# Scores and row maxima made one slot earlier in a fused threshold attention and gated MLP kernel

## The chip, the cores and the metric

The kernel runs on one core of a Trainium2 chip. The metric is the time of one execution on the device, in microseconds (us), taken as the median of several runs. Smaller is better.

## What is computed

The first half is attention over 8 batches of 8 heads, with 576 positions and a head size of 64, in which every score that lies more than `tau` below its row's maximum is thrown away before the softmax. The second half is a gated two-layer MLP on the 4608 rows that come out. The types are float32 at both ends.

```
def _attn_ref(q, k, v, tau):
    scale = 1.0 / np.sqrt(q.shape[-1])
    scores = scale * np.matmul(q, k.transpose(0, 1, 3, 2))
    thresh = np.max(scores, axis=-1, keepdims=True) - tau
    scores = np.where(scores >= thresh, scores, -1000000000.0)
    scores = scores - np.max(scores, axis=-1, keepdims=True)
    attn = np.exp(scores)
    attn = attn / (np.sum(attn, axis=-1, keepdims=True) + 1e-09)
    return np.matmul(attn, v).astype(np.float32)

def _moe_ref(x, w_in, w_out):          # x: [4608, 512], w_in: [512, 2048], w_out: [2048, 512]
    h = x @ w_in
    relu6 = np.clip(h + 3.0, 0.0, 6.0)
    g = h * relu6 / 6.0
    return (g @ w_out).astype(np.float32)
```

## The kernel before, in words

**Tiles.** Four heads make a *quad*, so there are 16 quads, two to a batch. A quad has nine *slots*: slots 0 to 3 are the four blocks of 128 query rows of its first pair of heads, slots 4 to 7 those of its second pair, and slot 8 holds the 64 left-over rows of all four heads. One slot is 128 rows by 576 keys for two heads. The loop runs over the 144 slots in order (`n` counts them), and each engine gets its instructions in the order in which this loop writes them: the schedule is written by hand, there is no planner. An engine works through its own list in order, so an instruction that waits holds up all that stand behind it.

**One pass of the loop** (slot `n`) writes, in this order:

- ScalarE: `sm_exp` (L315) of slot n-1, two heads;
- VectorE: `sm_max` (L302) of slot n, which copies the scores out of PSUM and takes their row maxima; GpSimd: the two `bias` values (L305) made from the maxima;
- TensorE: `mm1` (L378), the first MLP product of one item, into `ps_h`; then its relu (L387 on ScalarE or L389 on VectorE, chosen by slot through `on_act`) and its gate (L395, VectorE), which empties `ps_h`. Slot 8 has no `mm1`. An item is 320 columns wide (a *wide* slot) or 256 (a *narrow* one);
- TensorE, in the first 21 slots, for every second slot: `pe_transpose` of the weights of slot n-2, copied out by VectorE (L340);
- VectorE: `sm_recip` (L318) of slot n-1;
- TensorE: a quarter of an output tile (`mm2_part`, L407); the fourth quarter is followed by `osb` on VectorE (L415), which empties the one bank of `ps_o`;
- ScalarE: `sm_mask` (L310) of slot n, which needs the bias of slot n;
- by slot: transposes of queries and keys that later slots need, or `av_main` (L348) or `av_rest`. Queries are transposed by VectorE (L239) and keys too (L245) from quad 4 on; in quads 0 to 3 TensorE transposes them and VectorE or ScalarE copies them out (L237, L218, L220);
- TensorE: `scores` (L281, L287) of slot n+1;
- GpSimd: `sm_norm` (L323) of slot n-1; SyncE: the DMA transpose (L331) of its result;
- SyncE: a few loads of coming queries and keys, and finished output rows (L428); GpSimd: a few loads with a cast (weights, and values).

From quad 1 on the slot-dependent part was: second pair's queries in slot 1, its keys in slot 2, `av_main` in slots 3 and 8, `av_rest` in slot 4, the next quad's queries, keys and left-over rows in slots 5, 6 and 7.

**Buffers around the change.** The pool `ps_s` has two tiles of two PSUM banks each, and a slot's scores take both; so `scores` of one slot wait until `sm_max` of the slot before has read. `ps_h` has one tile: `mm1` of a slot waits for the gate of the slot before. The copy of the scores in SBUF (`s_pool`) has four buffers, and `sm_max` writes into one that `sm_norm` must have read. The DMA transposes and the loads stand in one list on SyncE.

**Start and end.** Before the loop, the first scores are made. During the first 22 slots there is no MLP work. After the loop, the rest of the MLP runs (`rest1`, `rest2`), with relu on ScalarE.

Of the kernel before, what the change touches and what calls it, by code (L numbers as in the profile page):

```python
# [21 lines left out]
def kernel(  # L22
# [17 lines left out]
    NQUAD = B * H // 4  # L40
    NSLOT = 9
    NB = 2
# [90 lines left out]
    def load_v(b):  # L133
        vm = v_pool.tile([P, H, 4 * D], BF16, tag="vm", name="vm")
        vr = vrs[b % 2]
        vsb[b] = (vm, vr)
        for g in range(2):
            vcasts.append(lambda g=g: nc.gpsimd.dma_start(
                out=vm[:, g * 4:g * 4 + 4, :],
                in_=v[b, g * 4:g * 4 + 4, 0:512, :].rearrange("h (p t) d -> p h (t d)", t=4)))  # L140
        for a in range(2):
            vcasts.append(lambda a=a: nc.gpsimd.dma_start(
                out=vr[a * 64:(a + 1) * 64, a, :, :],
                in_=v[b, :, 512:S, :].rearrange("(hp a) p d -> a p hp d", a=2)[a]))
# [21 lines left out]
    def start(jobs, n):  # L166
        for _ in range(min(n, len(jobs))):
            jobs.pop(0)()
# [30 lines left out]
    def qT_of(pair):  # L199
        return qkT[pair // 2][0][:, pair % 2, :]  # L200
# [68 lines left out]
    def keys(pair, a, hf):  # L269
        kT = kT_of(pair)  # L270
        c0 = 64 * (1 - a) + hf * HALF
        return kT[a * 64:(a + 1) * 64, c0:c0 + HALF]


    def scores(quad, slot):
        tiles = [ps_s.tile([P, 2, 512], F32, tag="s", name="s") for _ in range(2)]
        for hf in range(2):
            if slot < 8:
                pair, t = 2 * quad + slot // 4, slot % 4
                for a in range(2):  # L280
                    nc.tensor.matmul(tiles[a][:, hf, 0:HALF], qT_of(pair)[a * 64:(a + 1) * 64, t * P:(t + 1) * P],  # L281
                                     keys(pair, a, hf), start=True, stop=True)
            else:
                for n in range(2):
                    for a in range(2):
                        pair = 2 * quad + n
                        nc.tensor.matmul(tiles[a][n * 64:(n + 1) * 64, hf, 0:HALF],  # L287
                                         qT_of(pair)[a * 64:(a + 1) * 64, 512:S], keys(pair, a, hf),
                                         start=True, stop=True)
        return tiles  # L290
# [4 lines left out]
    def sm_max(sl):  # L295
        sl.s = s_pool.tile([P, 2, S], F32, tag="s", name="s")
        sl.m = stat_pool.tile([P, 2], F32, tag="m", name="m")
        sl.bias = stat_pool.tile([P, 2], F32, tag="bias", name="bias")
        sl.rsum = stat_pool.tile([P, 2], F32, tag="rsum", name="rsum")
        sl.rinv = stat_pool.tile([P, 2], F32, tag="rinv", name="rinv")  # L300
        for i, ps in enumerate(sl.tiles):
            nc.vector.tensor_scalar(out=sl.s[:, i, :].rearrange("p (a b) -> p a b", a=2), in0=ps[:, :, 0:HALF],  # L302
                                    scalar1=1.0, scalar2=None, op0=Alu.mult, op1=Alu.max,
                                    accum_out=sl.m[:, i:i + 1])
            nc.gpsimd.tensor_scalar(out=sl.bias[:, i:i + 1], in0=sl.m[:, i:i + 1], scalar1=-scale, scalar2=tau,  # L305
                                    op0=Alu.mult, op1=Alu.add)
# [6 lines left out]
    def sm_exp(sl, i):  # L313
        s = sl.s[:, i, :]
        nc.scalar.activation(out=s, in_=s, func=Act.Exp, accum_out=sl.rsum[:, i:i + 1])  # L315

    def sm_recip(sl):
        nc.vector.reciprocal(out=sl.rinv[:], in_=sl.rsum[:])  # L318
# [54 lines left out]
    def mm1(item, pool=None):  # L373
        b, ni, c0, w = item
        hps = (pool or ps_h).tile([P, 2, 512], F32, tag="s" if pool else "h", name="h")
        for n in range(2):
            for ki in range(KI):
                nc.tensor.matmul(hps[:, n, 0:w], w_in_sb[:, ki, (ni + n) * P:(ni + n + 1) * P],  # L378
                                 xT[b][:, ki, c0:c0 + w], start=(ki == 0), stop=(ki == KI - 1))
        return hps[:, :, 0:w]  # L380


    def mm1_relu(hps, on_act):
        w = hps.shape[2]
        r = r_pool.tile([P, 2, 320], F32, tag="r", name="r")[:, :, 0:w]
        if on_act:
            nc.scalar.activation(out=r, in_=hps, func=Act.Relu, bias=three[:])  # L387
        else:
            nc.vector.tensor_scalar(out=r, in0=hps, scalar1=3.0, scalar2=0.0, op0=Alu.add, op1=Alu.max)  # L389
        return r  # L390

    def mm1_gate(item, hps, r):
        b, ni, c0, w = item
        c0 += (b % 2) * S
        nc.vector.scalar_tensor_tensor(out=gbuf[:, ni:ni + 2, c0:c0 + w], in0=r, scalar=6.0, in1=hps,  # L395
                                       op0=Alu.min, op1=Alu.mult)
# [63 lines left out]
    queue = []  # L460
    for quad in range(NQUAD):
        for slot in range(NSLOT):
            sl = Slot()
            sl.quad, sl.slot = quad, slot
            sl.on_chip = len(queue) < N1 - 1 and len(queue) % 2 == 1
            queue.append(sl)
    queue[0].tiles = scores(0, 0)

    prev = None
    for n, sl in enumerate(queue):  # L470
        quad, slot = sl.quad, sl.slot
        b, g = divmod(quad, 2)
        now = n
        if slot in (0, 4):
            pts[2 * quad + slot // 4] = pt_pool.tile([P, 9, 512], BF16, tag="pT", name="pT")
        if slot == 8:
            ptr[quad] = ptr_pool.tile([P, 9, P], BF16, tag="pR", name="pR")
        if quad == 0 and slot == 0:
            load_quad(1)
        if slot == (4 if quad else 8) and quad + 2 < NQUAD:  # L480
            load_quad(quad + 2)
        if slot == 0 and g == 1 and b + 1 < B:
            load_v(b + 1)
        if prev is not None:
            for i in range(2):
                sm_exp(prev, i)
        sm_max(sl)

        if slot != 8 and todo1:
            item, then = todo1.pop(0)  # L490
            h = mm1(item)
            r = mm1_relu(h, on_act=(slot in ((1, 2, 3, 5, 6) if quad >= 2 * NB else (0, 1, 3, 5))))
            mm1_gate(item, h, r)
            todo2.extend(then)
        copies = pe_transpose(queue[n - 2]) if n > 1 and queue[n - 2].on_chip else None
        if prev is not None:
            sm_recip(prev)
        if copies:
            copies()
        outs = []  # L500


        pieces = 0 if slot == 3 else 1
        if slot == 0:
            second = True
        if second and slot < 2 and len(todo2) > 1 and todo2[0][1] == todo2[1][1]:
            pieces, second = 2, False
        for _ in range(pieces):
            if todo2:
                bb, mt, part = todo2.pop(0)  # L510
                mm2_part(bb, mt, part)
                if part == 3:
                    outs += mm2_out(bb, mt, on_act=False)
        for i in range(2):
            sm_mask(sl, i)
        evict = None
        nxt = 2 * quad + 2
        if slot == 1:
            evict = transpose_q(2 * quad + 1)
        elif slot == 2:  # L520
            evict = transpose_k(2 * quad + 1)
        elif n == 3:
            evict = transpose_rest(0, of_k=False)
        elif slot == 3 and quad > 0:
            av_main(2 * quad - 1)
        elif slot == 4 and quad > 0:
            av_rest(quad - 1)
            if quad % 2 == 0:
                todo1.extend(moe_of(quad // 2 - 1))
        elif slot in (5, 6, 7) and quad + 1 < NQUAD:  # L530
            if slot == 5:
                alloc_qk(quad + 1)
                evict = transpose_q(nxt)
            elif slot == 6:
                evict = transpose_k(nxt)
            else:
                evict = transpose_rest(quad + 1)
        elif slot == 8:
            av_main(2 * quad)
        if evict:  # L540
            evict()
        if n == 0:
            warm_up(8)
        if n + 1 < len(queue):
            queue[n + 1].tiles = scores(queue[n + 1].quad, queue[n + 1].slot)
        if n < 8:
            warm_up(6)
        if prev is not None:
            sm_norm(prev)
        flush()  # L550
        late.extend(outs)
        if not 30 < n < 34:
            start(loads, 1)
        if n < 4 or 15 < n < 20 or n > 33:
            start(vcasts, 1)
        elif n > 3:
            start(casts, 2 if 21 < n < 29 else 1)
        prev = sl
# [80 lines left out]
```

## Time and profile before

| | us |
|---|---|
| median of 5 runs | 550.01 |
| lowest and highest run | 548.73, 553.34 |
| the profiled execution's own time | 548.73 |
| its span in the profile | 547.0 |

| engine | busy us (share of the span) |
|---|---|
| TensorE, matmuls | 524.1 (96%) |
| TensorE, weight loads | 299.3 (55%) |
| ScalarE (ACT) | 463.0 (85%) |
| VectorE (DVE) | 428.8 (78%) |
| GpSimd (POOL) | 305.1 (56%) |

The page comes from one profiled execution. PE is TensorE, and matmul ends are modelled: matmuls overlap, so a busy PE is not a PE at its peak. A line such as L302 is a line of the kernel. In the timeline each row has its start, its length, the engine (a q after it means the engine's sequencer, so SPq is SyncE issuing a DMA), the line, what is written and read, and in brackets the idle time of the engine before it, with what ended it. In the list of waits the three numbers are the total, how often, and the longest.

### The profile page before, as it was taken

How to read it: one execution, taken by the hardware profiler on the slowest of the kernel's cores; microseconds unless marked ns; L12 is line 12 of the kernel's file. 1: busy time of each engine (PE TensorE's matmuls, PEld its weight loads, DVE VectorE, ACT ScalarE, POOL GpSimd, SP SyncE). 2: the span in 40 equal slices, each digit the busy share in tenths (PEclk: the TensorE clock that was granted, in tenths of full speed). 3: DMA queues.
4: the chain of work that ended last, by engine and by line, in shares of the span. 5: the costliest groups of instructions: out<-in, count | busy, mean ns of one | idle time of the engine just before them, and what ended most of it. 6: DMA issues, size and time to landing. Idle time of an engine off the chain costs nothing.

```text
span 547.0 us, 11518 instructions
## 1 busy us (share of the span) xinstructions
PE 524.1 (96%) x3774; PEld 299.3 (55%) x3774; DVE 428.8 (78%) x1055; ACT 463.0 (85%) x986; POOL 305.1 (56%) x646
## 2 busy tenths in 40 slices
PE   8998898999999999899999999999999999999997
PEld 7755465545555555555555555555555565554663
DVE  3888886788888888788988888888988888874441
ACT  4999989988989898999889899899889899993440
POOL 2888888666566555654566555754566555561000
PEclk9999999999999999999999999999999999999999
DMA  6999989989999997998699778998689786653102
GB/s 122 137 132 181 183 123 185 181 143 166 158 157 173 136 168 139 177 155 165 114 143 189 142 156 141 176 164 155 131 135 190 138 153 107 123 110 86 40 19 78
DMA packets 311692, 77.52 MB, mean 142 GB/s; under 512 B 294608, under 2 KB 307152, under 8 KB 311632
## 3 DMA queue, kind: packets, MB, share of 16 engines
q1 hardware_dynamic: 293024, 67.47, 70.1%
q0 software_dynamic: 17408, 8.92, 14.0%
q8 instruction: 30, 0.49, 0.4%
q10 hardware_dynamic: 1200, 0.39, 0.3%
q14 instruction: 30, 0.25, 0.2%
HBM read 36.70 MB, written 9.44 MB: 84 GB/s over the span
## 4 chain that ended last, share of the span: by engine, by line
PE 59%; ACT 10%; DVE 7%; POOL 4%; DMA 3%; issue 3%; SPq 1%; DVEq 0%; POOLq 0%
PE o L407 18%; PE h L378 17%; PE s L281 16%; ACT s L310 4%; PE av L348 4%; ACT s L315 3%; DVE s L302 3%; POOL pn L323 2%; DMA pR<-pn 2%; ACT r L387 2%; PE s L287 2%; DVE g L395 1%; DVE r L389 1%; DMA km<-in_k_dram 1%; PE av L351 1%
## 5 line engine op out<-in xcount | busy, mean ns | idle before, releaser
L323 POOL TENSOR_SCALAR pn<-s,rinv 128x576 bf16<-128x576 f32 x288 | 211.6, 745 | 126.0 <-DVE rinv L318 60.9
L302 DVE TENSOR_SCALAR_CACHE_REDUCE s<-s 128x576 f32<-128x576 f32 x288 | 205.2, 749 | 30.6 <-PE s L281 22.4
L310 ACT ACTIVATE s<-s,bias 128x576 f32<-128x576 f32 x288 | 206.9, 766 | 26.3 <-POOL bias L305 25.9
L315 ACT ACTIVATE s<-s 128x576 f32<-128x576 f32 x288 | 192.4, 670 | 0.3
L281 PE MATMUL s<-kT,qT 64*128 64x288 f32 x1024 | 172.2, 430 | 4.5 <-DVE s L302 4.2
L378 PE MATMUL h<-xT,w_in_sb 128*128 128x320 bf16 (+1 forms) x1024 | 145.0, 287 | 3.6 <-DVE g L395 2.8
L407 PE MATMUL o<-w_out_sb,g 128*128 128x512 bf16 x576 | 140.9, 379 | 3.9 <-DVE osb L415 3.9
L281 PEld LDWEIGHTS s<-kT,qT 64*128 64x128 f32 x1024 | 96.0, 186 | 65.8 <-DVE s L302 34.6
L378 PEld LDWEIGHTS <-w_in_sb 128*128 128x128 bf16 x1024 | 91.7, 98 | 66.3 <-issue 38.1
L395 DVE SCALAR_TENSOR_TENSOR g<-r,h 128x512 bf16<-128x512 f32 (+1 forms) x128 | 96.3, 754 | 37.7 <-ACT r L387 36.3
L305 POOL TENSOR_SCALAR bias<-m 128x1 f32<-128x1 f32 x288 | 54.4, 189 | 62.5 <-DVE s L302 41.1
L407 PEld LDWEIGHTS <-g 128*128 128x128 bf16 x576 | 55.6, 98 | 58.3 <-issue 9.9
L387 ACT ACTIVATE r<-h,three 128x640 f32<-128x640 f32 (+1 forms) x86 | 62.8, 732 | 25.7 <-PE h L378 25.3
L315 ACT ACTIVATION_READ_ACCUMULATOR s<-s 128x1 f32 x288 | 54.1, 188 | 0.0
L415 DVE TENSOR_SCALAR osb<-o 128x512 f32<-128x512 f32 x31 | 20.9, 674 | 21.7 <-PE o L407 21.4
L348 PE MATMUL av<-pT,vm 128*64 128x512 bf16 x256 | 33.7, 385 | 1.1 <-DMA pT<-pn 1.1
L348 PEld LDWEIGHTS <-vm 128*64 128x64 bf16 x512 | 17.6, 110 | 26.4 <-issue 13.3
L389 DVE TENSOR_SCALAR r<-h 128x512 f32<-128x512 f32 (+1 forms) x42 | 31.5, 750 | 0.0
L318 DVE RECIPROCAL rinv<-rsum 128x2 f32<-128x2 f32 x144 | 22.9, 159 | 8.4 <-ACT s L315 7.7
L360 DVE CAST xT<-av 128x512 bf16<-128x512 f32 x32 | 21.8, 681 | 6.6 <-PE av L351 6.5
L302 DVE DVE_READ_ACCUMULATOR s<-s 128x1 f32 x288 | 23.9, 83 | 0.0
L287 PE MATMUL s<-kT,qT 64*64 64x288 f32 x256 | 21.3, 415 | 0.6 <-DVE s L302 0.6
(57 smaller groups left out, 218.6 us busy)
## 6 DMA issues: line engine op xcount, KB each, us to landing
out_dram<-osb SPq DMA_DIRECT2D x31, 256.0 KB, 2.6
nq<-in_q_dram SPq DMA_DIRECT2D x96, 72.0 KB, 3.1
km<-in_k_dram SPq DMA_DIRECT2D x96, 64.0 KB, 2.7
vm<-in_v_dram POOLq DMA_DIRECT2D x16, 256.0 KB, 5.3
km<-in_k_dram SPq DMA_DIRECT2D x16, 128.0 KB, 4.2
w_in_sb<-in_moe_w_in_dram POOLq DMA_DIRECT2D x16, 128.0 KB, 4.4
w_out_sb<-in_moe_w_out_dram POOLq DMA_DIRECT2D x16, 128.0 KB, 4.2
pT<-pn SPq DMA_TRANSPOSE x119, 3.7
```

The lines of the kernel that those rows point to most:

```text
L281: nc.tensor.matmul(tiles[a][:, hf, 0:HALF], qT_of(pair)[a * 64:(a + 1) * 64, t * P:(t + 1) * P], keys(pair, a, hf), start=True, stop=True)
L302: nc.vector.tensor_scalar(out=sl.s[:, i, :].rearrange("p (a b) -> p a b", a=2), in0=ps[:, :, 0:HALF], scalar1=1.0, scalar2=None, op0=Alu.m ...
L305: nc.gpsimd.tensor_scalar(out=sl.bias[:, i:i + 1], in0=sl.m[:, i:i + 1], scalar1=-scale, scalar2=tau, op0=Alu.mult, op1=Alu.add)
L310: nc.scalar.activation(out=s, in_=s, func=Act.Prelu, bias=sl.bias[:, i:i + 1], scale=scale, alpha=REJECT)
L315: nc.scalar.activation(out=s, in_=s, func=Act.Exp, accum_out=sl.rsum[:, i:i + 1])
L323: nc.gpsimd.tensor_scalar(out=pn[:, i, :], in0=sl.s[:, i, :], scalar1=sl.rinv[:, i:i + 1], scalar2=1.0, op0=Alu.mult, op1=Alu.mult)
L348: nc.tensor.matmul(ps[a * 64:(a + 1) * 64, :], vm[:, 2 * hp + a, c * D:(c + 1) * D], pT[:, 5 * a + c, cols], start=(c == 0), stop=False)
L378: nc.tensor.matmul(hps[:, n, 0:w], w_in_sb[:, ki, (ni + n) * P:(ni + n + 1) * P], xT[b][:, ki, c0:c0 + w], start=(ki == 0), stop=(ki == KI ...
L387: nc.scalar.activation(out=r, in_=hps, func=Act.Relu, bias=three[:])
L389: nc.vector.tensor_scalar(out=r, in0=hps, scalar1=3.0, scalar2=0.0, op0=Alu.add, op1=Alu.max)
L395: nc.vector.scalar_tensor_tensor(out=gbuf[:, ni:ni + 2, c0:c0 + w], in0=r, scalar=6.0, in1=hps, op0=Alu.min, op1=Alu.mult)
L407: nc.tensor.matmul(o_ps[0], gbuf[:, ni, mt * P:(mt + 1) * P], w_out_sb[:, ni, :], start=(ni == 0), stop=(ni == NI - 1))
```

## The change

In the loop, `sm_max` now works on slot n+1 and `scores` on slot n+2, while `sm_mask` stays on slot n and `sm_exp` on slot n-1. The scores and maxima of slot 0 and the scores of slot 1 stand ahead of the loop. So that the operands of the scores are there, every transpose of queries and keys moves forward by one slot (0, 1 and 4, 5, 6 in place of 1, 2 and 5, 6, 7; in quad 0 the second pair's stay in slots 1 and 2). `av_main` and `av_rest` stay, so slot 4 now holds `av_rest` and a transpose of queries. The slots in which ScalarE does the relu change: from quad 4 on 0, 1, 3, 4, 5 in place of 1, 2, 3, 5, 6, and in the quads before 0, 2, 3, 4 in place of 0, 1, 3, 5; in the others VectorE does it.

```diff
     queue[0].tiles = scores(0, 0)
+    sm_max(queue[0])
+    queue[1].tiles = scores(0, 1)
...
         if prev is not None:
             for i in range(2):
                 sm_exp(prev, i)
-        sm_max(sl)
+        if n + 1 < len(queue):
+            sm_max(queue[n + 1])
 
         if slot != 8 and todo1:
             item, then = todo1.pop(0)
             h = mm1(item)
-            r = mm1_relu(h, on_act=(slot in ((1, 2, 3, 5, 6) if quad >= 2 * NB else (0, 1, 3, 5))))
+            r = mm1_relu(h, on_act=(slot in ((0, 1, 3, 4, 5) if quad >= 2 * NB else (0, 2, 3, 4))))
             mm1_gate(item, h, r)
...
-        if slot == 1:
+        if n == 1 or slot == 0 and quad > 0:
             evict = transpose_q(2 * quad + 1)
-        elif slot == 2:
+        elif n == 2 or slot == 1:
             evict = transpose_k(2 * quad + 1)
         elif n == 3:
             evict = transpose_rest(0, of_k=False)
...
-        elif slot in (5, 6, 7) and quad + 1 < NQUAD:
-            if slot == 5:
+        if slot in (4, 5, 6) and quad + 1 < NQUAD:
+            if slot == 4:
                 alloc_qk(quad + 1)
                 evict = transpose_q(nxt)
-            elif slot == 6:
+            elif slot == 5:
                 evict = transpose_k(nxt)
             else:
                 evict = transpose_rest(quad + 1)
-        elif slot == 8:
+        if slot == 8:
             av_main(2 * quad)
...
-        if n + 1 < len(queue):
-            queue[n + 1].tiles = scores(queue[n + 1].quad, queue[n + 1].slot)
+        if n + 2 < len(queue):
+            queue[n + 2].tiles = scores(queue[n + 2].quad, queue[n + 2].slot)
```

## The prediction, made before the changed kernel ran

> **What bounds the kernel now.** I read the busy times first, then the windows of 20 us (start:end, length, then PE, PEld, DVE, ACT and POOL busy), then waits and timeline.
>
> ```profile
> 20.00:40.00 20.00, 19.40 (x144) 12.06 (x143) 16.57 (x48) 19.07 (x43) 16.48 (x36) 1.00 0.98 141
> 80.00:100.00 20.00, 16.37 (x117) 10.33 (x118) 14.15 (x40) 18.81 (x41) 17.04 (x36) 1.00 1.30 189
> 380.00:400.00 20.00, 19.97 (x156) 10.46 (x154) 17.92 (x45) 18.40 (x42) 11.50 (x26) 1.00 0.75 148
> ```
>
> There are three regimes. Until about 72 us (slots 0 to 21) TensorE has filler transposes in it and ScalarE is the full engine. From 72 to 120 us nobody is full. From there to 490 us TensorE is, with ScalarE and VectorE at 90% close behind. A plain slot of the third regime:
>
> ```profile
> 265.36 1.24 PE L281 MATMUL s<-kT,qT 64*128 64x288 f32 x8
> 266.53 1.26 PE L378 MATMUL h<-xT,w_in_sb 128*128 128x320 bf16 x8
> 267.63 1.03 PE L407 MATMUL o<-w_out_sb,g 128*128 128x512 bf16 x4
> 268.58 1.24 PE L281 MATMUL s<-kT,qT 64*128 64x288 f32 x8
> ```
>
> Each group starts before the one before it is drained: 3.22 us from scores to scores, no hole. A narrow plain slot takes 3.01. Taking each slot's length (scores start to next scores start) less the shortest slot of the same content gives TensorE's stalls: 6.2 us in slots 23 to 35, 12.2 us in slots 36 to 142. No change of order can save more than that there.
>
> What the change cuts is ScalarE's wait for the bias (here over the whole span), and the second line shows the loop that ties TensorE to relu and gate:
>
> ```profile
> ACT s L310 <- POOL bias L305: 25.9, 60, 2.3
> DVE g L395 <- ACT r L387: 36.3, 77, 2.3
> PE h L378 <- DVE g L395: 2.8, 5, 0.8
> ```
>
> By windows, the 25.9 us are 4.4 before 72 us (2.3 of them before the first mask), 5.5 from 72 to 122, 15.5 from 122 to 490. A second queue binds too, SyncE's:
>
> ```profile
> 87.14 2.01 SPq L124 DMA_DIRECT2D kr<-in_k_dram  x2
> 89.25 1.72 SPq L331 DMA_TRANSPOSE pT<-pn  x1
> 91.02 3.15 SPq L97 DMA_DIRECT2D km<-in_k_dram  x4
> 94.28 1.83 SPq L331 DMA_TRANSPOSE pT<-pn  x1
> 99.25 1.05 PE L348 MATMUL av<-pT,vm 128*64 128x512 bf16 x8 [0.85 <-DMA pT<-pn]
> 230.19 0.32 PE L348 MATMUL ar<-pR,vm 128*64 128x64 bf16 x8 [1.31 <-DMA pR<-pn]
> ```
>
> From 76 to 103 us SyncE issues without a pause. The transpose at 94.28 is of a slot whose normalisation ended at 88.4, 5.9 us before, and TensorE waits for it. `av_rest` in slot 4 of the odd quads 3, 5, 7, 9, 11 and 13 starts within 0.14 us of its transpose's landing, each time.
>
> **What the Trainium skill says.**
> - Perfetto Trace Analysis, Identifying the Most-Contended Engine: matmul busy time is no measure of TensorE's headroom. So I use the slot lengths, not the 96%.
> - PSUM — Partial Sum Buffer, Specifications (TRN2): 8 banks. The pools take 4 (scores), 2 (`ps_h`), 1 and 1, so the scores cannot be double buffered, and making them a slot earlier gives no second buffer. The trace agrees: scores wait for the VectorE copy (34.6 us of PEld waits for L302).
> - ScalarE: Activation LUTs, What ACT_TABLE_LOAD costs: an ACTIVATE with pointer bias is 280 + 0.833 N ns, back-to-back ones overlap by 93. For N = 576 that is 760, the trace has 766 (exp: 670). Undisturbed, mask to mask reads 2.68 us in the trace.
> - Perfetto Trace Analysis, DMA Instruction — HWDGE: the issuing sequencer is held from the wait's end until the descriptors are generated. The trace agrees: 1.3 to 3.1 us per transpose, and what follows on SyncE waits.
>
> **The change, part by part.** Instruction counts hardly change; order does. On TensorE and VectorE `scores` and `sm_max` stand where they stood, named one slot later, so their ping-pong over `ps_s` is as before. SyncE's list is unchanged, and GpSimd's is but for two biases ahead of the loop and the order at its end. What changes:
>
> 1. *Bias a slot early, first 22 slots.* Mask(0) starts at 9.65, mask(22) at 72.72: 63.07 us for 22 slots, against 22 × 2.68 = 59.0 if ScalarE never waits, so at most 4.1; the waits shown are 4.4 − 2.3 = 2.1. VectorE needs about 21.5 us per nine slots, under 24.1; filler gives TensorE room. I take **−3.0**, and give back 0.5 because DMA already runs at 181 to 183 GB/s from 41 to 68 us and `av_main` in slot 26 has only 1.7 us of slack to its transpose: **−2.5** (ends 0 and −4.1).
> 2. *Slots 22 to 35.* mask(22) to mask(36) takes 48.7 us against 14 × 2.68 + 4 relus × 0.56 + 2.1 of key copies ≈ 42 on ScalarE, which looks like −6. But `av_main` in slot 30 and `av_rest` in 31 end SyncE's chain, which starts with the transpose at 74.94 and is as long as before; it starts earlier by what part 1 gave. So up to slot 31 nothing more. In slots 32 to 35 stalls go from 1.35 to about 1.05: **−0.3** (ends +0.5 and −4).
> 3. *Slots 36 to 142.* Waits for the bias cost only where they delay a relu, hence a gate, hence `mm1`. I count about 2.5 us of the 12.2 as such (0.54 in slot 121, 0.64 in 106, 0.40 in 70, and smaller). Against that, relu on VectorE moves to slots 2, 6, 7 from 0, 4, 7. Slots 0 and 4 were long (3.88 to 4.09 with two pieces of `mm2`, 3.45 to 3.66 with `av_rest`), slot 2 is plain. In a VectorE-relu slot, counted from `mm1`'s start at 259.45:
>
> ```profile
> 259.64 0.76 DVE L302 TENSOR_SCALAR_CACHE_REDUCE s<-s 128x576 f32<-128x576 f32 x1
> 261.00 0.82 DVE L389 TENSOR_SCALAR r<-h 128x640 f32<-128x640 f32 x1
> 261.86 0.82 DVE L395 SCALAR_TENSOR_TENSOR g<-r,h 128x640 bf16<-128x640 f32 x1
> ```
>
> The gate ends at +3.23, and 0.05 later the next `mm1` can start (so after 414.41, at 414.46): 3.28 against a plain 3.23. Every 0.1 us by which VectorE comes late into such a slot is now a stall, where a ScalarE relu forgives up to 0.75. It comes late after a key transpose (0.70 long; +0.2), and by 0.7 to 0.9 when an `osb` (0.60) is in that slot too. Writing the nine slots in a row with these durations (gate spacing 0.60 narrow, 0.74 wide), I get per quad, by where `osb` falls: slots 1, 7 (quads 4, 5): 1.8 each; 1, 6 (6, 10, 14): 0.5; 0, 5 (7, 11): 0.7; 0, 4, 8 (8, 12): 0.4; 2, 7 (9, 13): 0.9; quad 15: 0.2; and 1.4 for quad 7's DMA wait. Sum 10.7 against 12.2. Half of that lies ahead of an `av_rest` that SyncE times anyway, so **−0.6** (ends +8.4 and −5).
> 4. *Slot 4 takes a query transpose (0.76) beside `av_rest`'s copy (0.28)*: the slot is 3.45 or more, VectorE needs about 3.5. Nothing; if cover fails, 0.2 in each of 12 quads, within part 3's ends.
> 5. *Buffers of s*: `sm_max` of slot m now needs the norm of slot m−4 with one slot less in hand: 5.5 − 3.4 ≈ 2 us left. Nothing; where GpSimd is late by 2 us, it costs what is over.
> 6. *The end.* At 494.47 `mm1` waits 0.81 for a gate, whose relu stood behind mask and exp of slot 143; that mask had waited 0.53 for its bias. Also 24 matmuls at 490.23 took 0.16 too long. **−0.7** (ends 0 and −1).
>
> Sum: −2.5 − 0.3 − 0.6 − 0.7 = **−4.1 us**. The profiled execution took 548.73 (span 547.0), so 544.6 for its like; it was the fastest of five, and the median is 1.28 higher: 545.9, rounded to **545.8**.
>
> **Rivals.**
> - *VectorE's relu in short slots becomes the bound (slower).* Place: gate to next `mm1` in slots 2 and 6, quads 4 to 15. Price if VectorE is 0.45 late there in wide and 0.25 in narrow slots: 12 × 2 × 0.35 = 8.4. Less 3.5 (start and end) and 2 of stalls gone, 550 + 2.9 = 553. It decides from about 0.3 us lateness in each. For it: VectorE at 90%, late by 0.2 after each key transpose. Against: TensorE has 0.10 spare in slot 6, and no `mm1` follows slot 7.
> - *SyncE and DMA set the pace (no change).* The start's gain is eaten by the 76 to 103 us chain, and later ones by `av_rest`. Left is the end: 549.3. For it: zero slack in six quads. Against: the chain's start is itself timed by a norm that comes earlier.
> - *Shorter waits shorten SyncE's chain too.* Start 3.0, slots 22 to 35 3.5, later 3, end 0.7: 10.2, so 539.8. Against: transposes late by 4 to 6 us in every odd quad.
>
> **How the numbers follow.** Forecast 0.45 (543 to 548.5), slower rival 0.22, no change 0.20, larger gain 0.13. A measurement of this kernel can tell about 0.5% (2.75 us) from no change. Faster: 0.40 + 0.13 = 0.53; same: 0.05 + 0.20 = 0.25; slower: 0.22. The range leaves out half the larger gain and the upper half of the slower case: 540.0 to 553.5; forecast alone 543 to 548.5.
>
> **What would show it.** Part 1: mask(22) near 70. Part 2: no idle of mask for bias, yet `av_main` of slot 30 waits longer for its transpose. Part 3: new `mm1` waits for the gate in slots 2, few in 3; plain slots still 3.01 and 3.23. Part 6: the 0.81 gone. Wrong if plain slots lengthen, if mask(22) stays near 72.7, or if `av_main` of slot 30 comes over 4 us earlier.

## The result, and the profile after

The changed kernel takes **552.74 us** (median of 29 runs, 550.66 to 555.92) against 549.95 us for the kernel before in the same rounds: ratio **1.0049, 95% interval [1.0036, 1.0062]**. It is slower by about 0.5%, where 545.8 us was forecast. Its profiled execution took 554.44 us, with a span of 552.7 (548.73 and 547.0 before).

The windows of 20 us that were shown of before, with one of 12 us put in (columns as there; PEclk is the third number from the end):

```profile
20.00:40.00 20.00, 18.69 (x155) 12.49 (x155) 15.45 (x46) 17.98 (x40) 14.96 (x33) 1.00 0.94 147
80.00:100.00 20.00, 18.57 (x130) 11.98 (x129) 16.42 (x45) 18.86 (x43) 16.61 (x36) 1.00 1.21 160
100.00:112.00 12.00, 5.58 (x31) 2.89 (x30) 3.43 (x10) 4.51 (x11) 5.54 (x12) 0.72 1.30 176
380.00:400.00 20.00, 20.00 (x147) 11.12 (x144) 18.21 (x46) 18.54 (x41) 10.81 (x23) 1.00 0.78 140
```

In the first row ScalarE (fourth busy time) fell from 19.07 to 17.98: it was to be kept full and has more holes than before. The last row is as before. The third row has no counterpart above; this is the line of before:

```profile
100.00:112.00 12.00, 11.66 (x94) 6.46 (x90) 9.98 (x24) 10.51 (x24) 7.08 (x15) 1.00 1.18 173
```

From 100 to 112 us TensorE now works 5.6 of 12 us, at 0.72 of its clock, where it worked 11.7 at full clock. The waits:

```profile
DVE g L395 <- ACT r L387: 28.1, 78, 1.9
PE av L348 <- DMA pT<-pn: 6.4, 1, 6.4
ACT s L310 <- POOL bias L305: 6.0, 12, 2.3
PE h L378 <- DVE g L395: 3.0, 8, 0.7
```

ScalarE's wait for the bias went from 25.9 to 6.0 us, so the change does what it says. But all of that was cut from 72 us on: ahead of it the wait is 5.5 (4.4 before). And there is one new wait of 6.4 us, that of `av_main` in slot 30. What released it, from SyncE's timeline:

```profile
79.00 2.10 SPq L331 DMA_TRANSPOSE pT<-pn  x1
...
90.62 2.71 SPq L331 DMA_TRANSPOSE pT<-pn  x1
...
94.83 2.04 SPq L331 DMA_TRANSPOSE pT<-pn  x1
96.91 3.94 SPq L97 DMA_DIRECT2D km<-in_k_dram  x4
100.95 2.48 SPq L331 DMA_TRANSPOSE pT<-pn  x1
103.47 2.74 SPq L92 DMA_DIRECT2D nq<-in_q_dram  x4
106.30 2.05 SPq L331 DMA_TRANSPOSE pR<-pn  x1
```

and TensorE's:

```profile
99.39 1.03 PE L378 MATMUL h<-xT,w_in_sb 128*128 128x256 bf16 x8 [0.38 <-DVE g L395]
106.84 1.92 PE L348 MATMUL av<-pT,vm 128*64 128x512 bf16 x8 [6.42 <-DMA pT<-pn]
108.55 0.64 PE L351 MATMUL av<-pT,vr 128*64 128x512 bf16 x2
109.12 2.02 PE L281 MATMUL s<-kT,qT 64*128 64x288 f32 x8
111.07 1.05 PE L378 MATMUL h<-xT,w_in_sb 128*128 128x256 bf16 x8
```

Three things are to be seen. SyncE's full stretch starts at 79.00, 4.06 us later than before (74.94). It is longer: from there to the landing of slot 25's transpose at 106.80 it takes 27.8 us, before 24.2 (74.94 to 99.11). The norm of slot 25 had ended at 92.02, so its transpose, issued at 100.95, stood 8.9 us in SyncE's list (5.9 before). And after the idle TensorE runs at half its clock: the eight `av` matmuls take 1.92 us, before 1.05, and the scores behind them 2.02, else 1.24; at 111.07 `mm1` is at full speed again.

The start, from TensorE's timeline and from ScalarE's:

```profile
18.33 1.24 PE L281 MATMUL s<-kT,qT 64*128 64x288 f32 x8 [0.78 <-DVE kT L218]
24.36 0.66 PE L230 MATMUL tp<-identf,nq 128*128 128x128 f32 x4 [1.13 <-DMA nq<-in_q_dram]
```

```profile
73.53 1.44 ACT L310 ACTIVATE s<-s,bias 128x576 f32<-128x576 f32 x2
```

The last is mask(22): 73.53, before 72.72, forecast 70. A plain slot of the third regime, in which nothing has changed (3.23 us from scores to scores, 3.01 in a narrow one):

```profile
271.18 1.24 PE L281 MATMUL s<-kT,qT 64*128 64x288 f32 x8
272.36 1.26 PE L378 MATMUL h<-xT,w_in_sb 128*128 128x320 bf16 x8
273.45 1.03 PE L407 MATMUL o<-w_out_sb,g 128*128 128x512 bf16 x4
274.41 1.40 PE L281 MATMUL s<-kT,qT 64*128 64x288 f32 x8
```

`av_main` and `av_rest` stand in the same slot in every version, so the start of their matmuls can be laid side by side: us of before, and how much later each kernel comes (one profiled execution each; the last four columns are from the experiments below; `late` and the two fills have the list of before up to slot 26 and still come 0.2 to 0.95 later there, a difference made in the first 9 us).

| at | before | changed | late | transposes | fill27 | fill27_warm |
|---|---|---|---|---|---|---|
| slot 26 | 82.72 | +4.08 | +0.88 | +3.56 | +0.20 | +0.95 |
| slot 30 | 99.25 | +7.60 | +1.10 | +3.94 | +2.66 | +1.55 |
| slot 31 | 103.78 | +9.13 | +1.30 | +4.06 | +2.34 | +4.74 |
| slot 40 | 136.39 | +8.97 | +4.35 | +3.38 | +2.09 | +6.11 |
| slot 139 | 476.81 | +7.44 | +3.30 | +2.27 | -0.05 | +3.12 |
| end | 546.95 | +5.72 | +1.58 | +2.27 | -1.77 | +1.41 |

So the changed kernel loses 4.1 us by slot 26, 3.5 more at slot 30 and 1.5 more at slot 31 (half clock), and wins back 3.4 after that. These are two single executions, 5.7 us apart where the medians are 2.8 apart, so the column shows where time goes and overstates how much a middling run loses.

### The profile page after: what moved, and what is told of

The parts are those of the page before. It is cut to its first block, busy times and chain, and to the rows that moved or that the text cites. A ratio compares the mean times of both kernels' runs of the same rounds, so it can differ in the third digit from the quotient of the medians.

```text
span 552.7 us, 11551 instructions
## 1 busy us (share of the span) xinstructions
PE 524.2 (95%) x3774; PEld 299.5 (54%) x3774; DVE 431.1 (78%) x1056; ACT 460.4 (83%) x985; POOL 305.1 (55%) x646
## 4 chain that ended last, share of the span: by engine, by line
PE 59%; DVE 10%; ACT 8%; DMA 6%; issue 3%; POOL 1%; DVEq 0%; POOLq 0%
PE h L378 18%; PE o L407 17%; PE s L281 16%; PE av L348 4%; DVE s L302 4%; DMA pR<-pn 3%; ACT s L315 3%; ACT s L310 3%; DMA pT<-pn 2%; DVE g L395 2%; ACT r L387 2%; DVE r L389 2%; PE s L287 1%; DVE osb L415 1%; PE av L351 1%
```

## The experiments

The theories: **A**, the loss is made ahead of slot 31, by the extra slot of scores at the start and SyncE's stretch behind it, and the order itself is no worse; **B**, relu on VectorE in slots 2, 6 and 7 costs it; **C**, the transposes that stand a slot earlier wait for loads. Ratios are to the kernel before in the same rounds.

**1. New order late, new order early.** `late` has the order of before up to slot 35 and makes one extra slot of scores at the end of slot 35; `early` is the mirror of it.

```diff
-        if n + 1 < len(queue):
+        if n < N0:
+            sm_max(sl)
+        elif n + 1 < len(queue):
             sm_max(queue[n + 1])
...
+        if n < N0:
+            queue[n + 1].tiles = scores(queue[n + 1].quad, queue[n + 1].slot)
+        if n == N0 - 1:
+            sm_max(queue[N0])
-        if n + 2 < len(queue):
+        if n >= N0 - 1 and n + 2 < len(queue):
             queue[n + 2].tiles = scores(queue[n + 2].quad, queue[n + 2].slot)
```

(Against the changed kernel; the maxima and second scores ahead of the loop are out. N0 = 36; transposes and relu slots go over at the same slot.)

> The order of the kernel before up to slot 35, the new order (scores, maxima, transposes, relu slots) from slot 36 on. Theory A (the whole loss is made ahead of slot 31: one more slot of scores to fill at the start, and SyncE's chain behind it; from slot 36 on the new order is 1 to 2 us better): av_main of slot 30 near 99 us as before, 548.5 us in all, ratio to before 0.995 to 1.000. Theory B (relu on VectorE in slots 2, 6, 7 costs in the steady part): 552 to 553 us, ratio 1.004 to 1.006. Theory C (transposes that stand a slot earlier wait for loads, in every quad): 551 to 552 us.

Measured: 550.0 us, ratio 0.9997 [0.998, 1.0014].

> The mirror of that: the new order up to slot 35, the order of before from slot 36 on (slot 36 has no scores of its own to make, since they are there). Theory A: av_main of slot 30 near 106.8 us as in the changed kernel, 554 us in all, ratio 1.006 to 1.010. Theory B: 550 us, ratio 0.999 to 1.001. Theory C: between, 551 to 552 us.

Measured: 556.62 us, ratio 1.012 [1.0086, 1.0155]; `av_main` of slot 30 at 105.23, its eight matmuls again 1.92 us long. The loss lies in the early slots, as A has it, and B and C miss both. Yet `early` came out slower than A said as well: in its profile, the slowest of its six runs, 3.8 us more go between slots 48 and 53, in the old order, at a wait of 2.44 us for SyncE's transpose and at half clock from 179 to 182 us. And `late` does not gain either: between slots 35 and 39 it loses 3.2 us (from +1.13 to +4.35), and wins 2.8 back later. The extra slot has a price here too.

**2. Relu slots alone, transposes alone.**

```diff
-            r = mm1_relu(h, on_act=(slot in ((1, 2, 3, 5, 6) if quad >= 2 * NB else (0, 1, 3, 5))))
+            r = mm1_relu(h, on_act=(slot in ((0, 1, 3, 4, 5) if quad >= 2 * NB else (0, 2, 3, 4))))
```

> The kernel before with the new relu slots alone. Theory A: no difference that can be measured, 549.5 to 551 us. Theory B: the whole loss, 552.5 us, ratio 1.004 to 1.006. Theory C: 550 us.

Measured: 553.26 us, ratio 1.0051 [1.0025, 1.0077]: as B said, and against A. TensorE's waits from 120 to 490 us, first of before, then of this kernel:

```profile
PE h L378 <- DVE g L395: 0.4, 1, 0.4
```

```profile
PE h L378 <- DVE g L395: 2.8, 11, 0.4
```

In the old order `mm1` does wait for gates behind a relu on VectorE. Is that so in the new order? The changed kernel with the old relu slots:

> The changed kernel with the relu slots of the kernel before. The new relu slots alone cost 0.5% in the old order; open is whether they cost it in the new order too. Theory A (the loss stands at the start and in SyncE's chain, and the relu slots are matched to the order they stand in): no gain, 552 to 557 us, ratio to before 1.004 to 1.012. Theory B (the relu slots are the loss): 549 to 550.5 us, ratio 0.998 to 1.002.

Measured: 551.05 us, ratio 1.0025 [1.0004, 1.0046]. With the old ones in quads 0 to 3 alone (the edit is the second tuple only):

> The changed kernel with the relu slots of before in quads 0 to 3 alone (slots 23 to 35), the new ones after that. All relu slots set back gave 551.0 us, ratio 1.0025. If that came from the slots ahead of 36 (less of VectorE in SyncE's stretch): 550.5 to 551.5 us, ratio 1.001 to 1.004. If from the later ones: 552 to 553.5 us, ratio 1.004 to 1.007.

Measured: 551.86 us, ratio 1.0033 [1.0012, 1.0054]. Both lie between the two cases, and their intervals overlap the changed kernel's. At most a part of the loss is in the relu slots, and if so, in the early ones; for those from quad 4 on experiment 6 has a cleaner comparison. The profiled execution with all old relu slots, which took 548.29 us, is 5.8 us late at slot 26, more than the changed kernel, but 4.9 at slot 30 without a half clock there, and 0.4 us early at the end.

> The kernel before with the transposes of queries and keys a slot earlier, as in the changed kernel, and scores and maxima where they were. Theory A: at most the wait for quad 1's queries in slot 4 (1.1 us), of which little reaches slot 30: 550 to 551 us, ratio 1.000 to 1.002. Theory B: 550 us. Theory C: the whole loss, 552.5 us, ratio 1.004 to 1.006.

(The edit is the transpose part of the change, in the kernel before.) Measured: 550.75 us, ratio 1.0002 [0.9986, 1.0019]. In its profile the first transpose of quad 1's queries waits for its load:

```profile
22.15 0.68 PE L230 MATMUL tp<-identf,nq 128*128 128x128 f32 x4 [1.92 <-DMA nq<-in_q_dram]
```

and the clock is at half from 22 to 26 us (and again from 94 to 97); at slot 26 it is 3.56 us late, at the end 2.27. So C is a real cost at the start, larger than I expected in that execution, and the earlier transposes win 1.8 us of it back after slot 31. That is about half of what the changed kernel wins back there.

**3. Two edits on the start of the changed kernel.** Quad 0's transposes in slots 5, 6, 7 again:

```diff
-        if slot in (4, 5, 6) and quad + 1 < NQUAD:
-            if slot == 4:
+        if slot in ((4, 5, 6) if quad else (5, 6, 7)) and quad + 1 < NQUAD:
+            if slot == (4 if quad else 5):
...
-            elif slot == 5:
+            elif slot == (5 if quad else 6):
```

> The changed kernel, but in quad 0 the transposes for quad 1 stay in slots 5, 6 and 7, so that they don't wait for loads. Theory A: av_main of slot 8 near 34.2 us (35.7 in the changed kernel, 31.7 before), what is left over before being the one slot of scores to fill, 2.4 us; the chain of SyncE starts as much earlier, 551.2 us in all, ratio 1.001 to 1.004. If the first loads don't matter: 552.7 us, ratio 1.004 to 1.006. Theory B: 552.7 us.

Measured: 552.9 us, ratio 1.0051 [1.0033, 1.0069]; `av_main` of slot 8 at 36.73, not 34.2. The wait for the load is gone, but now the scores of slot 9 wait 0.64 us for the keys' copy, and VectorE's maxima 0.70 and 0.94 us for a norm. The start has more than one late operand, and freeing one moves the wait to the next. With experiment 2 this separates the two things that stand early at the start: the early transposes without the extra slot cost nothing that can be measured in all (1.0002), and the extra slot with quad 0's transposes put back costs the whole loss (1.0051). Five buffers for the SBUF copy of the scores:

```diff
-    s_pool = ctx.enter_context(tc.tile_pool(name="sp", bufs=4))
+    s_pool = ctx.enter_context(tc.tile_pool(name="sp", bufs=5))
```

> The changed kernel with five buffers for the SBUF copy of the scores, not four. Theory A: VectorE's waits for a norm (1.9 us ahead of 75 us, 3.0 later) go, of which little reaches the slots: 551.5 to 553 us, ratio 1.003 to 1.006. Rival S (the buffers hold the start up, since the maximum of slot m now waits for the norm of slot m-4 with one slot less in hand): av_main of slot 8 at 33.5 us or earlier (35.7 in the changed kernel), 548.5 to 550.5 us, ratio 0.997 to 1.001.

Measured: 553.95 us, ratio 1.0064 [1.0039, 1.0088]; `av_main` of slot 8 at 36.03. The buffers are not it.

**4. SyncE's stretch.** Quad 4's loads two slots earlier in the list:

```diff
-        if slot == (4 if quad else 8) and quad + 2 < NQUAD:
+        if slot == (2 if quad == 2 else 4 if quad else 8) and quad + 2 < NQUAD:
```

> The changed kernel, but the loads of quad 4 are put in line from slot 2 of quad 2 on, two slots earlier, so that two of SyncE's five jobs of loads are issued ahead of its full stretch. Theory A (SyncE's chain sets av_main of slot 30, and TensorE comes out of the long idle at half its clock): av_main of slot 30 comes 3 to 6 us earlier, at 101 to 104 us, TensorE's clock stays at 1.0, 547.5 to 549.5 us in all, ratio 0.995 to 1.000. Rival (the transfers themselves are what is late, not their issue): av_main of slot 30 within 1.5 us of 106.8, ratio 1.003 to 1.006. Theory B: 552.7 us.

Measured: 551.97 us, ratio 1.0016 [0.9987, 1.0045]. The median misses what was expected; the single runs tell more. The three with a mean clock of 1.0 took 546.9 to 547.4 us, six with 0.990 to 0.994 552.1 to 553.9 (a seventh, at 556.1, does not count in the ratio). Together with the edit of quad 0:

> The changed kernel with both: quad 0's transposes in their old slots and quad 4's loads two slots earlier. Theory A: the two add up, 546 to 548 us, ratio 0.992 to 0.997. If the start doesn't matter once the chain is short: as with the loads alone. Theory B: 552.7 us.

Measured: 551.9 us, ratio 1.0001 [0.9966, 1.0036]. Here too: six of 14 runs have a clock of 0.999 or 1.0 and a median of 547.4 us, seven one of 0.994 or less and 553.3. In the profiled execution, one of the first kind, `av_main` of slot 30 comes at 102.84 after a wait of 1.09. So the stretch can be shortened this way; that it is not in every run is read from the clocks alone. A stronger edit: quad 4's queries and keys loaded in the row form of quads 0 to 3. SyncE then issues 12 loads for them in place of 18, and the elements of quad 4 stand in another order than its transposes take them for, so these two kernels leave out putting quad 4's elements in order, and only their times are of use.

```diff
-            if b < NB:
+            if quad <= 2 * NB:
```

(in `load_k`, `load_q` and the choice in `rest`.)

> The changed kernel with the queries and keys of quad 4 loaded row by row, as those of quads 0 to 3 are, and not in blocks of 32 (so the elements of quad 4 stand in another order than its transposes take them for; nothing else is changed). SyncE issues 12 loads for it in place of 18, in longer pieces. Theory A (SyncE's full stretch sets slot 30): the stretch from the transpose of slot 21 to the landing of slot 25's is 19 to 23 us (27.8 in the changed kernel), av_main of slot 30 at 98 to 103 us, the clock at 1.0, 544 to 548 us in all, ratio to before 0.990 to 0.997. Rival (norms or the casts' transfers set it): av_main of slot 30 later than 105 us, ratio 1.003 to 1.006.

Measured: 548.18 us, ratio 0.9963 [0.9942, 0.9984]. The stretch takes 22.7 us (79.46 to 102.17), and slot 30:

```profile
102.21 1.05 PE L348 MATMUL av<-pT,vm 128*64 128x512 bf16 x8 [1.34 <-DMA pT<-pn]
```

> The same loads of quad 4 in the kernel before, as the control. There slot 30 waits 0.85 us for its transpose. Theory A: little to gain, 547.5 to 550 us, ratio 0.996 to 1.000, so that the two orders come out level or the new one 1 to 3 us ahead. If the plain loads help every order alike (less traffic): 544 to 547 us, and the new order stays 2 to 3 us behind.

Measured: 549.5 us, ratio 0.9985 [0.9971, 0.9999]; here slot 30 no longer waits for a transpose:

```profile
99.58 1.05 PE L348 MATMUL av<-pT,vm 128*64 128x512 bf16 x8 [0.60 <-ACT kT L220]
```

The new order gains 4.6 us of median from that edit, the old one 0.5 to 0.9. With a short stretch the new order is not behind (1.3 us ahead, though the two intervals overlap). This is what A said. The profile of the new order with that edit also shows that the late start is not yet the loss: it is 4.5 us late at slot 26, more than the changed kernel, but 3.0 at slot 30 and 0.4 us early at the end. In these profiles a late start became a loss where the stretch was long and the clock fell behind it.

**5. The half clock.** Fillers in the wait of slot 30 of the changed kernel:

```diff
         elif slot == 3 and quad > 0:
+            if n == 30:
+                warm_up(26)
             av_main(2 * quad - 1)
```

> The changed kernel with 26 filler transposes of the identity on TensorE ahead of av_main of slot 30, inside the wait for SyncE's transpose. They shorten no wait; they only keep TensorE busy. Theory A (a part of the loss is TensorE's clock, which falls to half after the idle of 6.4 us): av_main of slot 30 at 106 to 107 us as before, but its matmuls take 1.05 us and not 1.92, the clock of the run is 0.997 or more, 1.5 to 2.5 us less, 550.2 to 551.3 us in all, ratio to before 1.000 to 1.003. If the clock costs nothing: 552.7 us or more, ratio 1.004 to 1.006.

Measured: 555.86 us (7 runs), ratio 1.0092 [1.0059, 1.0125]. At the place it did what was expected:

```profile
102.49 3.06 PE L181 MATMUL warm<-identf 128*128 128x128 f32 x26 [2.20 <-DVE g L395]
105.48 1.05 PE L348 MATMUL av<-pT,vm 128*64 128x512 bf16 x8
...
236.63 0.32 PE L348 MATMUL ar<-pR,vm 128*64 128x64 bf16 x8 [2.42 <-DMA pR<-pn]
```

Slot 31 came 3.2 us earlier than in the changed kernel, 1.4 of that already at slot 30, whose transpose landed earlier in this run. The third line is where it was given back in this execution: a wait for SyncE in slot 67, and half clock from 238 to 241. It is the fastest of the seven, at 553.32 us, so it does not show what made the others slower. The runs' clocks lie between 0.987 and 0.997, as those of the changed kernel do. With quad 4's loads early as well:

> The changed kernel with quad 4's loads put in line two slots earlier (which alone gave two groups of times, near 547 us at a clock of 1.0 and near 552.5 at 0.990 to 0.997) and the 26 fillers ahead of av_main of slot 30. Theory A: the slow group goes, 546.5 to 549 us, ratio to before 0.994 to 0.999. If the clock is a symptom and no cause: two groups as before, ratio 0.999 to 1.004.

Measured: 557.02 us (7 runs), ratio 1.0104 [1.0068, 1.014]. The transpose of slot 25 had landed at 101.75, and the fillers held `av_main` until 106.30; two half-clock stretches came later. Both runs missed. Fillers ahead of a wait of unknown length were no remedy here; why half clock came later in both profiles stays open.

**6. The extra slot at another place.** The switch of experiment 1, but with N0 = 27, so that the extra scores stand at the end of slot 26, which has no `mm1`. Relu slots: old in quads 0 to 3, new from quad 4 on.

> The order of before up to slot 26 and the new order from slot 27 on: the one slot of scores that has to be made ahead is made at the end of slot 26, where TensorE has no MLP product and will wait for SyncE's transposes anyway. Relu slots: those of before in quads 0 to 3, the new ones from quad 4 on. Theory A (the loss is where the extra slot is filled: at the start it delays the norms that start SyncE's full stretch, and nothing gives the time back before slot 31): av_main of slot 30 at 99 to 101 us, the stretch not longer than before, and the gain of the later slots is kept: 545.5 to 548 us, ratio to before 0.992 to 0.997. Rival F (an extra slot costs its 2.4 to 3.2 us wherever it is filled, as at slot 36): slot 31 at 106.5 to 108 us, 549 to 550.5 us, ratio 0.998 to 1.001. Theory B (the new relu slots): 551 to 553 us.

Measured: **547.44 us, ratio 0.9956 [0.9938, 0.9973]**: faster than both kernels; `av_main` of slot 30 at 101.91, a little later than expected. The edit moves the extra slot and, for quads 0 to 2, the early transposes with it. With the old relu slots throughout:

> The order of before up to slot 26, the new order from slot 27 on, and the relu slots of before throughout. Theory A: as with the new relu slots from quad 4 on, within 1 us: 545.5 to 548.5 us, ratio 0.992 to 0.998. Theory B (in the steady part the new relu slots cost): 1 to 2.5 us less than with the new ones. If the new relu slots are what makes the new order gain in the steady part: 1 to 3 us more than with them.

Measured: 546.7 us (5 runs), ratio 0.9952 [0.9939, 0.9964]. In the new order the relu slots from quad 4 on cost at most 0.7 us, which is hardly clear of the noise of 10 and 5 runs; those of quads 0 to 3 are old in both. In the profile of the first, the extra scores:

```profile
84.51 2.06 PE L281 MATMUL s<-kT,qT 64*128 64x288 f32 x8 [0.32 <-DVE s L302]
88.26 2.96 PE L281 MATMUL s<-kT,qT 64*128 64x288 f32 x8 [1.69 <-DVE s L302]
91.15 1.89 PE L378 MATMUL h<-xT,w_in_sb 128*128 128x256 bf16 x8
```

They stand 1.69 us for the maximum, and then the clock is at half until about 94 us (2.96 us for scores that else take 1.24 to 2.06). So fillers went there, where the length of the wait is set by VectorE:

```diff
         if n == N0 - 1:
+            warm_up(14)
             sm_max(queue[N0])
```

> The kernel that goes over to the new order at slot 27 (547.4 us, ratio 0.9956, its clock at 0.5 from 88 to 94 us after TensorE had stood for 1.69 us between the two groups of scores at the end of slot 26), with 14 filler transposes of the identity in that gap. Theory A, with the half clock as a cost of its own: no half clock from 88 to 94 us, av_main of slot 30 at 99.5 to 101 us (101.9 without the fillers), 545 to 546.8 us in all, ratio to before 0.991 to 0.995. If the half clock costs nothing, or SyncE's stretch takes the gain back: 547 to 548 us, ratio 0.995 to 0.997.

Measured: **545.82 us, ratio 0.9927 [0.99, 0.9954]**. The same place:

```profile
87.25 1.75 PE L181 MATMUL warm<-identf 128*128 128x128 f32 x14
89.00 1.91 PE L281 MATMUL s<-kT,qT 64*128 64x288 f32 x8
90.85 1.05 PE L378 MATMUL h<-xT,w_in_sb 128*128 128x256 bf16 x8
```

The half clock at this place is gone. That the fillers shorten the whole run is not shown: the intervals of the two kernels overlap. From slot 26 to slot 30 the kernel with fillers loses 0.6 us to the kernel before, 2.5 without the fillers. Its profiled execution, at 550.14 us the slowest of its eight, waited 3.44 us for SyncE's transpose in slot 31 and was at half clock after it; that is the +4.74 of the table. Five of the eight runs have a clock of 0.999 or 1.0, and took 544.7 to 545.9 us.

## Why the prediction was wrong, point by point

**Part 1 (the first 22 slots, -2.5) is the step that failed**: 3.0 of the 4.1 us that would be gone "if ScalarE never waits" were to be saved, more than the 2.1 us of waits that it had counted, because "filler gives TensorE room". Instead of 2.5 us gained, 4.1 were lost by slot 26 in the profiled execution. Mask(22) came at 73.53 and not near 70. The working took 2.68 us a slot, ScalarE's own pace, and asked only whether VectorE has the busy time for it. But in these slots a bias comes when VectorE has its maximum, that when TensorE has made the scores, and those when their operands are there; made a slot earlier, they meet late loads and late copies (0.78 and 1.13 us above). The pace stayed near 2.9 us, and ScalarE waited 5.5 us instead of 4.4. The two lines that make the first scores and maxima ahead of the loop had no term in the sum at all. In the profile they have: by the start of the scores that end each pass of the loop, the changed kernel is 2.35 us behind in pass 1, 3.25 in pass 2 (key copy), 4.0 in pass 5 (after the query load).

**Part 2 (-0.3)** named the right chain and took its sign from part 1: SyncE's stretch "starts earlier by what part 1 gave". It starts when the norm of slot 21 ends, and the norm ends with the pass of the loop, not with the mask: 4.06 us later. Slot 21's exponentials, its reciprocal and its norm, first before, then changed:

```profile
72.06 0.19 ACT L315 ACTIVATION_READ_ACCUMULATOR s<-s 128x1 f32 x1
72.99 0.16 DVE L318 RECIPROCAL rinv<-rsum 128x2 f32<-128x2 f32 x1
73.45 1.47 POOL L323 TENSOR_SCALAR pn<-s,rinv 128x576 bf16<-128x576 f32 x2
```

```profile
73.33 0.19 ACT L315 ACTIVATION_READ_ACCUMULATOR s<-s 128x1 f32 x1
75.69 0.76 DVE L302 TENSOR_SCALAR_CACHE_REDUCE s<-s 128x576 f32<-128x576 f32 x1 [0.55 <-PE s L281]
77.05 0.16 DVE L318 RECIPROCAL rinv<-rsum 128x2 f32<-128x2 f32 x1
77.50 1.47 POOL L323 TENSOR_SCALAR pn<-s,rinv 128x576 bf16<-128x576 f32 x2
```

ScalarE is done only 1.3 us later than before. The other 2.8 us are VectorE's list: the reciprocal of slot 21 stands behind the maximum of slot 23, and is taken 3.5 us after its input is there (0.7 before). So the change lets the mask run ahead of the rest of its pass, and leaves behind the result that SyncE waits for. No run wrote the reciprocal ahead of the maximum, so what that would give is open.

That the stretch would also be 3.6 us longer, and that TensorE would come out of the wait at half clock (1.5 us), was not foreseen either. Instead of -2.8, parts 1 and 2 made +9.1 by slot 31. Why the same list of SyncE took 27.8 us here, 23.7 with the old relu slots (experiment 2) and 26.9 with quad 0's transposes back (experiment 3) is not settled; experiment 4 shows only that fewer issues make it short.

**Part 3 (-0.6)** was about right. The stalls of slots 36 to 142 went from 12.2 to 11.2 us. New waits of `mm1` for a gate are there (1.8 us from 120 to 490 us, 0.4 before), plain slots did not lengthen, and a relu on VectorE ahead of a wide slot reads 3.29 from `mm1` to `mm1` (261.84 to 265.13) where 3.28 was worked out. What it did not see: the earlier transposes alone win 1.8 us (experiment 2).

**Parts 4 and 5 (nothing)** held from slot 36 on, and the fifth buffer gained nothing anywhere. In quad 0, part 4 had not asked whether the load of quad 1's queries lands a slot earlier; it does not.

**Part 6 (-0.7)** was right in sign, and 1.7 us in size from slot 139 to the end: the last passes have no scores to make, which is the extra slot of the start coming back.

**The rivals.** "SyncE and DMA set the pace" named the place, but expected the start's gain to be eaten there, not a loss at the start to be enlarged. The slower rival gave the right side of the result (553) by luck, for another reason: relu in short slots costs 0.5% in the old order, and in the new one, from quad 4 on, nothing that is clear of noise. The signs listed as fatal were the right ones: mask(22) near 72.7 was among them. Slot 30 was watched for a start over 4 us earlier; that it could come 7.6 us later was not asked.

## What to carry to other kernels

A stage that is made to run one step ahead needs one more step of work before the first result, and everything that stands behind it in program order comes later by that; put a price on it, and put it where the engine waits anyway: here 4 us at the start, 3.2 in the full slots, 0.6 in a slot without an MLP product, its gap filled (2.5 with the gap open), each from one profiled execution. Ask, too, which results the moved step now stands ahead of in its engine's list. A late start on the path to a saturated queue can become a longer wait, so follow the moved step to the queue's first entry, not to the engine it was meant to relieve.

## What was not expected of the hardware

TensorE's clock falls to half after short idles too. Half clock for some 3 to 7 us followed, among others, listed idles of 6.42 (changed kernel), 4.76 (`early`), 2.42 (slot 67 with fillers), 1.92 and 1.35 (transposes alone, at 22 and 94 us) and 1.69 us (fill at slot 26). It did not follow 2.33 us (relu slots set back, slot 30), 1.60 us (changed kernel at 179) or 1.31 us (before at 230). And it came at 73 us with the relu slots set back, and at 61 us with five buffers and with the old relu slots in quads 0 to 3, after a listed idle of only 0.28 or 0.29, with one of 0.93 to 0.99 some 2.5 us ahead of it. A listed idle is the last gap alone; whether several short ones add up was not tested. The Trainium skill (TensorE: Matmul & The Clock Gate, HAM oscillation — how this bites in real kernels) gives idle gaps of over about 3.4 us as the ones to avoid; these runs show it after gaps of 1.35 us and less, so shorter gaps aren't safe. A run's mean clock then tells much of its time: in 59 runs of the kernel before, 29 with a clock of 0.999 or 1.0 have a median of 549.25 us, 27 with 0.995 to 0.998 one of 551.06, and three with 0.994 or less one of 553.0. No run of the changed kernel was above 0.997. Sorted like this the two kernels lie close: the changed one has 551.57 us in 10 runs at 0.995 to 0.997 and 553.14 in 19 at 0.994 or less. What it lacks is the full-clock runs. This is a sorting and no proof of cause, since a wait that lowers the clock costs time itself.
